# Block-sparse attention and a gated MLP in one kernel: transposing the probabilities of 28 jobs and of the all-key groups with VectorE blocks and transfers within SBUF

## The chip, the cores and the metric

One core of one Trainium2 chip runs the whole program in one launch. The metric is the device time of one execution in microseconds (us). A time of the program is the median of several executions; the profile is of one more execution, and it has a time of its own.

## What is computed

The inputs are q, k and v of shape (4, 8, 768, 64): 4 batches, 8 heads, 768 tokens, 64 columns, in float32. Tokens are cut into 24 blocks of 32. A query block attends to the blocks beside it, to the first and the last block, and to 3 sampled blocks; the first and the last query block attend to all 24. The attended rows go through an MLP without bias, with a gate.

```python
scores = scale * np.matmul(q, k.transpose(0, 1, 3, 2))
mask = np.abs(blk_i - blk_j) <= window
mask = mask | (blk_i == 0) | (blk_j == 0) | (blk_i == n_blocks - 1) | (blk_j == n_blocks - 1)
for qb in range(n_blocks):
    for kb in sampled_blocks[qb]:
        mask[qb * block:(qb + 1) * block, kb * block:(kb + 1) * block] = True
...
attn = np.exp(scores)
attn = attn / (np.sum(attn, axis=-1, keepdims=True) + 1e-09)
attn_out = np.matmul(attn, v)
...
h = x @ w_in            # (3072, 512) @ (512, 2048)
g = h * np.clip(h + 3.0, 0.0, 6.0) / 6.0
out = g @ w_out         # (3072, 2048) @ (2048, 512)
```

## The kernel before

**Units of work.** Attention is done in 24 groups (`GROUPS`), each of two batches and two query blocks. 22 of them are sparse: a group gives two jobs (class `Job`, L452), one for each batch, so there are 44 jobs, numbered 0 to 43. A job holds 2 query blocks of all 8 heads against 8 key blocks each. The two other groups hold the first and the last query block, which see all keys: each gives four pieces of dense work (class `Dense`, L536), so there are 8, numbered 0 to 7. A dense piece works in two halves of 384 keys.

**A job, step by step.** `s` (L462) writes scores with TensorE into two PSUM banks; `mx` takes the negated maxima with VectorE; `e` (L479) is four exponentials of ScalarE of 128x256, which write the probabilities `p` with the keys of a chunk interleaved (an inner step of 4 elements). Probabilities then stand with queries on the partitions, and the product with V needs keys there. So `t` (L486) turns them: four TensorE transposes of 128x128 against `ident` into a third PSUM bank, twice per job, and `ca` (ScalarE) or `cv` (VectorE) copies each bank to SBUF as `pT`. `av` (L499) multiplies with V: 16 small matmuls of 32 output rows each, twice per job, into the bank `small` (the trace shows each of these float32 matmuls, and those of `s`, as two). `dn` and `ml` divide, `x` transposes the 128x256 result in blocks of 32x32 with VectorE, `xh` and `xl` split it into two parts of float32r for the MLP.

**A dense piece** has the same steps, with four sets of three transposes (`t`, L572, twice per half) and `av` with 64 output rows per matmul. Its `x` (L617) is 8 small TensorE matmuls against `ident` into `small` (16 in the trace).

**The MLP** is 96 steps (class `Step`, L658): 6 units of 512 tokens by 16 slices of the hidden width. `h` is 12 matmuls of 128x512 in two halves, `o` 12 more in four parts. `wh` (ScalarE) and `wl` (GpSimd, now and then VectorE) split a weight slice; `ga`, `gb`, `gh`, `gl` make the gated hidden slice and split it. A unit starts when 4 groups of attention are done. Weights are loaded and unpacked once, in 32 pieces (class `Weight`), in the first 200 us or so. Keys and values of a group are gathered into one of two `kp` and `vp` buffers (class `Cache`, L377; `RING = 2`).

**What sets the order.** The order is written out by hand in one list, `SCORE` (L44): phrases such as `j36 e_10 e_11` name the work and its operations. Every operation is issued in this order through a helper at L316, so each engine runs its own operations strictly in the list's order, and nearly every row of a trace has the line L316. Most transfers go through one queue, SyncE's (SP). Where an operation on an engine waits, everything behind it on that engine waits too.

**Buffers the change touches.** `p` and `pT`: 3 buffers of 512 columns each. `WBUFS = (3, 2)`: buffers of the split `w_in` and `w_out` slices. `EARLY = 4`: jobs of the first 4 groups use the banks that `o` needs later (`OUT`) for scores and transposes.

Of the kernel before, what the change touches and what calls it, by code (L numbers as in the profile page):

```python
# [10 lines left out]
F32 = mybir.dt.float32  # L11
# [3 lines left out]
ALU = mybir.AluOpType  # L15
# [19 lines left out]
EARLY = 4  # L35
WBUFS = (3, 2)
# [8 lines left out]
    k0 samp_1; q1 load_0; k0 table_1; c0 kg_0; q0 load_1; c1 vw_01; c0 kw_11 vg_0; w1 load_1; c0 kr_111 kr_001; c1  # L45
    kw_11 vw_00 kf_0; c0 vw_01 kw_00; c1 kc_1; k0 index; w0 load_0; c1 kr_000; w1 size; q0 qs_0; c1 kr_010; c0 vw_02
    vw_00; k0 ident_0; c0 vr_01; j1 s; j0 s; j1 mx_0; c0 vr_00; j1 mx_1; c2 kc_0; j0 mx_0; w0 size; j0 mx_1; j1 e_00;
    c1 vr_00; w0 bits_0; j0 e_00 e_01; j1 e_01; j0 e_10; c1 vw_02; j0 e_11; q1 qs_0; w2 load_0; c2 kr_010; j2 s; j0
    t_0 t_1; c2 kr_000; j0 cv_0 ca_1; j1 t_0; j0 av_0; j1 e_10 cv_0 e_11; j0 av_1; j2 mx_0; c2 kw_01; j3 s; j0 dn; j2
    e_00; j0 ml; j2 e_01 mx_1; j1 t_1; c3 kw_01; j3 mx_0; j2 t_0; c1 vg_0; w0 bits_1; q2 load_0; j1 av_0; j2 ca_0; c1  # L50
    vr_01; j3 mx_1; j2 e_10; j1 cv_1; j3 e_00; j2 e_11; w1 bits_0; j1 av_1; j3 e_01; w1 bits_1; w2 size; j2 t_1; c2
    vw_00; w0 bits_2; c3 kr_010; j2 ca_1; j1 dn; j0 x; j3 e_10; j1 ml; w1 bits_2; j1 x; q3 load_0; c2 vw_02; q2 qs_0;
    w4 load_0; m0 wh_0; j4 s; c2 vr_01; j3 e_11; m0 wl_00; j1 xh; m0 wh_1; j2 av_0; j1 xl_1; c2 vw_01; j0 xh; j5 s; c3
    kc_1; c2 vr_00; w2 bits_0; j3 t_0; j5 mx_0; c3 kr_000; j3 t_1; j0 xl_1; j5 e_00; j2 av_1; j4 mx_0 e_00; j2 dn; q3
    qs_0; j2 ml; q4 load_0; j3 ca_0 cv_1; j4 e_01; j3 av_0; w2 bits_1; w4 size; j3 av_1; j2 x; j5 e_01; m0 wl_11; j4
    t_0; c3 vw_00; j4 mx_1; c4 kw_01; j4 ca_0; w3 load_0; j3 dn; j4 e_10; c3 vr_01; w2 bits_2; j4 e_11; j3 ml; j4 t_1;
    j5 mx_1; j4 av_0; c3 vw_01; j4 cv_1; j5 t_0; c3 vw_02; j3 x; c3 vr_00; j6 s; j5 e_10; j2 xh; j5 e_11; j2 xl_0; j5
    ca_0; j4 av_1; c4 kw_00; j6 mx_0; c4 kr_000; j5 t_1; w4 bits_0; j6 e_00; j4 dn; j6 e_01; j7 s; j5 cv_1; j3 xh; w3
    size; j6 mx_1 t_0; c4 kr_010; j4 ml; j6 e_10; j3 xl_1; j5 av_0; j6 ca_0; j7 mx_0; j6 e_11; j5 av_1; w3 bits_0; j7
    e_00; w3 bits_1; j7 e_01; w6 load_0; j7 t_0; w3 bits_2; j6 t_1; j5 dn; j7 mx_1; j4 x; j7 e_10; w4 bits_1; j6 ca_1;  # L60
    q4 qs_0; j5 ml; w4 bits_2; j6 av_0; j7 ca_0; j6 av_1; j5 x; j7 e_11; w5 load_0; j4 xh; j7 t_1; c5 kw_00; j6 dn; j5
    xh; j4 xl_0; c4 vw_01; j6 ml; j7 ca_1; j8 s; w7 load_0; j5 xl_0; j6 x; m1 wh_0; c4 vw_02 vw_00; j7 av_0; j6 xh; m1
    wl_00; j8 mx_0; c4 vr_00; m2 wh_0; j7 av_1; j8 e_00; j7 dn; j8 e_01; j7 ml; j8 t_0; c4 vr_01; j7 x; j6 xl_1; j7
    xh; w6 size; j7 xl_1; j8 mx_1; m0 h_0; w5 size; j8 e_10; w5 bits_0; j8 e_11; w6 bits_0; m0 h_1; m1 wh_1; j8 cv_0;
    m1 wl_11; j8 t_1; m0 ga; w6 bits_1; j8 ca_1; w6 bits_2; j9 s; m0 gb; w9 load_0; q5 load_0; w5 bits_1; m0 gh; m1
    h_0; c5 kw_01; w5 bits_2; w7 size; m0 gl; j9 mx_0; w8 load_0; m1 h_1; c5 kr_000; m2 wl_01; j9 e_00 e_01; w7
    bits_0; m0 o_0; m1 ga; j8 av_0; m1 gb; w9 size; j8 av_1; c5 kr_010; j9 mx_1; m3 wh_0; j9 t_0; m2 h_0; w7 bits_1;
    m3 wl_00; j9 e_10 e_11; w7 bits_2; m1 gh; m0 o_1; m1 gl; m2 h_1; w9 bits_0; w10 load_0; c5 vw_00 vw_01; m0 o_2; j8
    dn; m2 ga; w9 bits_1; m0 o_3; w8 size; w9 bits_2; j9 t_1 ca_0; m1 o_0; j8 ml; w11 load_0; q5 qs_0; j9 cv_1; c5
    vr_01; m1 o_1; w8 bits_0; j10 s; m2 gb; c6 kw_00; m2 gh; j9 av_0; c5 vw_02; j10 mx_0; m2 wh_1; j9 av_1; m2 gl; c5  # L70
    vr_00; j10 mx_1; m1 o_2; w10 size; w8 bits_1; j10 e_00; m1 o_3; j10 e_01; m2 wl_11; j10 e_10; m3 h_0; j10 e_11; w8
    bits_2; w10 bits_0; m4 wh_0; w12 load_0; m3 h_1; j8 x; w11 size; w10 bits_1; j10 t_0; m4 wl_01; m3 ga; m2 o_0; w10
    bits_2; j10 t_1; j9 dn; w14 load_0; m2 o_1; w11 bits_0; j10 ca_1; m3 gb; m2 o_2; j8 xh; j10 ca_0; w11 bits_1; m4
    h_0; m5 wh_0; j9 ml; w11 bits_2; m3 wh_1; j11 s; m3 gh; w13 load_0; c6 kr_010; m3 gl; j10 av_0; j11 mx_0; j10
    av_1; j11 mx_1; m4 h_1; j11 e_00; w12 size; m5 wl_01; j11 e_01; q6 load_0; m3 wl_11; j11 e_10; m2 o_3; c6 kr_000;
    m4 ga; w12 bits_0; m3 o_0; w14 size; m4 gb; m3 o_1; j11 e_11; w12 bits_1; m4 gh; j11 t_0; w12 bits_2; c6 kw_01; m5
    h_0; m4 gl; j11 ca_0; j10 dn; w16 load_0; j9 x; w13 size; c6 vr_01; j11 t_1; w13 bits_0; m5 h_1; w14 bits_0; j11
    ca_1; w14 bits_1; m4 wh_1; m3 o_2; w14 bits_2; m6 wh_0; j10 ml; m5 ga; m3 o_3; w15 load_0; m4 wl_11; q6 qs_0; j11
# [215 lines left out]
def fused_kernel(ctx: ExitStack, tc, qT, kG, vG, vP, kD, vD, sampled, w_in, w_out, table, ident_d, out):  # L294
# [42 lines left out]
    class Index(Work):  # L337
# [99 lines left out]
    class Group(Work):  # L437
# [347 lines left out]
```

## Time and profile before

| what | value |
|---|---|
| median of 3 executions | 771.0 us (770.13 to 771.55) |
| the profiled execution's own time | 768.11 us |
| its span, from first to last instruction | 766.3 us |
| TensorE busy | 724.3 us, 95% of the span |
| VectorE / ScalarE / GpSimd busy | 45% / 56% / 47% |
| granted TensorE clock, mean of the span | 0.994 |
| moved by DMA | 102.52 MB, mean 134 GB/s |

The profiled execution is 2.9 us below the median of the others. Busy time counts an instruction from its start to its modelled end; TensorE's instructions overlap, so what a matmul costs is read from the distance between the starts of neighbours, not from its own duration. `PE` is TensorE's matmul, `PEld` its weight load, DVE is VectorE, ACT ScalarE, POOL GpSimd, SP the queue of SyncE.

### The profile page before, as it was taken

How to read it: one execution, taken by the hardware profiler on the slowest of the kernel's cores; microseconds unless marked ns; L12 is line 12 of the kernel's file. 1: busy time of each engine (PE TensorE's matmuls, PEld its weight loads, DVE VectorE, ACT ScalarE, POOL GpSimd, SP SyncE). 2: the span in 40 equal slices, each digit the busy share in tenths (PEclk: the TensorE clock that was granted, in tenths of full speed). 3: DMA queues.
4: the chain of work that ended last, by engine and by line, in shares of the span. 5: the costliest groups of instructions: out<-in, count | busy, mean ns of one | idle time of the engine just before them, and what ended most of it. 6: DMA issues, size and time to landing. Idle time of an engine off the chain costs nothing.

```text
span 766.3 us, 18861 instructions
## 1 busy us (share of the span) xinstructions
PE 724.3 (95%) x7616; PEld 558.4 (73%) x7616; DVE 341.7 (45%) x698; ACT 426.4 (56%) x790; POOL 360.7 (47%) x291
## 2 busy tenths in 40 slices
PE   1577999999999999999999999999999999999997
PEld 0344777777777777777778777777777777888885
DVE  2567989895443434542323334436642133221112
ACT  1567678766565445645656554455654645544441
POOL 0011324355446434455664663442546564676663
PEclk9989999999999999999999999999999999999999
DMA  8688878776361553223451144533442600010001
GB/s 281 199 274 253 284 232 246 239 249 198 122 197 62 169 176 124 64 74 115 153 161 58 35 138 129 179 131 106 133 142 86 207 20 2 1 56 1 0 1 55
DMA packets 57866, 102.52 MB, mean 134 GB/s; under 512 B 7859, under 2 KB 36148, under 8 KB 57780
## 3 DMA queue, kind: packets, MB, share of 16 engines
q1 hardware_dynamic: 56512, 99.62, 41.3%
q10 hardware_dynamic: 1268, 1.71, 0.6%
q8 instruction: 60, 0.98, 0.5%
q14 instruction: 26, 0.21, 0.1%
HBM read 95.00 MB, written 6.29 MB: 132 GB/s over the span
## 4 chain that ended last, share of the span: by engine, by line
PE 89%; SPq 4%; DMA 2%; DVE 2%; ACT 1%; issue 1%; ACTq 0%; POOL 0%; POOLq 0%; DVEq 0%
PE hid L316 35%; PE out L316 34%; PE bank L316 12%; PE small L316 8%; SPq L316 3%; DMA stage<-w_out 1%; ACT p L316 1%; SPq L370 1%; DVE m L316 0%; DMA stage<-w_in 0%; DMA kp<-kG 0%; ACT g L316 0%; DMA vp<-vG 0%; DMA out_dram<-stage 0%; DVE w_in L316 0%
## 5 line engine op out<-in xcount | busy, mean ns | idle before, releaser
L316 PE MATMUL hid<-x,whi 128*128 128x512 f32 x768 | 242.9, 397 | 0.3 <-ACT x L316 0.2
L316 POOL TENSOR_TENSOR glo<-g,ghi 128x512 fp32r<-128x512 f32 x96 | 126.5, 1318 | 181.8 <-ACT ghi L316 163.6
L316 DVE SCALAR_TENSOR_TENSOR g<-g,hid 128x512 f32<-128x512 f32 x96 | 65.8, 686 | 229.8 <-ACT g L316 229.8
L316 PEld LDWEIGHTS hid<-x,whi 128*128 128x128 f32 x768 | 140.6, 188 | 34.6 <-issue 3.2
L316 POOL TENSOR_TENSOR wlo<-w_out,whi 128x512 fp32r<-128x512 f32 x87 | 113.7, 1308 | 98.0 <-ACT whi L316 78.3
L316 PE MATMUL out<-whi,ghi 128*128 128x512 f32 x384 | 159.7, 416 | 0.0
L316 ACT ACTIVATE p<-bank,m 128x256 f32<-128x256 f32 (+1 forms) x192 | 120.8, 691 | 65.1 <-DVE m L316 64.5
L316 POOL TENSOR_TENSOR wlo<-w_in,whi 128x512 fp32r<-128x512 f32 x87 | 113.4, 1308 | 84.3 <-ACT whi L316 79.7
L316 PE MATMUL out<-whi,glo 128*128 128x512 f32 x384 | 150.5, 392 | 0.2 <-POOL glo L316 0.2
L316 PE MATMUL hid<-x,wlo 128*128 128x512 f32 x384 | 150.2, 391 | 0.0
L316 PE MATMUL out<-wlo,ghi 128*128 128x512 f32 x384 | 150.0, 391 | 0.0
L316 ACT ACTIVATE g<-hid,half_b 128x512 f32<-128x512 f32 x96 | 66.1, 688 | 122.8 <-PE hid L316 93.1
L316 DVE TENSOR_REDUCE m<-bank 128x2 f32<-128x512 f32 (+1 forms) x112 | 70.3, 645 | 61.0 <-PE bank L316 60.9
L316 PEld LDWEIGHTS out<-whi,ghi 128*128 128x128 f32 x384 | 72.1, 188 | 22.9 <-issue 9.5
L316 PEld LDWEIGHTS out<-whi,glo 128*128 128x128 f32 x384 | 72.1, 188 | 16.5 <-POOL glo L316 0.6
L316 PEld LDWEIGHTS hid<-x,wlo 128*128 128x128 f32 x384 | 72.1, 188 | 15.8
L316 PEld LDWEIGHTS out<-wlo,ghi 128*128 128x128 f32 x384 | 72.4, 189 | 11.6
L316 ACT CAST whi<-w_out 128x512 fp32r<-128x512 f32 x96 | 60.0, 625 | 32.5 <-PE out L316 29.2
L316 ACT CAST ghi<-g 128x512 fp32r<-128x512 f32 x96 | 60.0, 625 | 31.9 <-DVE g L316 17.2
L316 ACT CAST whi<-w_in 128x512 fp32r<-128x512 f32 x96 | 59.6, 624 | 12.9 <-PE hid L316 8.3
L316 PE MATMUL bank<-ident,p 128*128 128x128 f32 x384 | 58.2, 274 | 2.0 <-ACT p L316 1.7
L316 PEld LDWEIGHTS small<-vp,pT 128*32 128x32 f32 x2816 | 42.6, 110 | 22.9 <-issue 15.3
(59 smaller groups left out, 607.4 us busy)
## 6 DMA issues: line engine op xcount, KB each, us to landing
vp<-vG SPq DMA_DIRECT2D x176, 130.0 KB, 3.4
kp<-kG SPq DMA_DIRECT2D x129, 128.0 KB, 2.8
kp<-kG SPq DMA_DIRECT2D x42, 256.0 KB, 3.6
stage<-w_in SPq DMA_DIRECT2D x16, 512.0 KB, 3.9
stage<-w_out SPq DMA_DIRECT2D x15, 512.0 KB, 4.3
vp<-vP SPq DMA_DIRECT2D x26, 260.0 KB, 3.9
stage<-vD SPq DMA_DIRECT2D x16, 390.0 KB, 4.0
out_dram<-stage SPq DMA_DIRECT2D x24, 256.0 KB, 2.9
```

The lines of the kernel that those rows point to most:

```text
L316: return lambda *a, **k: tc.keep_in_program_order(op(*a, **k))
L370: loads, values = nc.values_load_multi_w_load_instructions(row, engines=[engines[q]], min_val=0, max_val=NB - 1, skip_runtime_bounds_check ...
```

## The change

Jobs 16 to 43 (28 jobs, `MOVED = 16`) and all 8 dense pieces no longer use TensorE to turn the probabilities. `e` writes into one tile `p` of 1024 columns, with the 4 slots of a chunk outermost. `tr` (VectorE) transposes each 32x32 block in place, in two instructions of 128x512 per job (128x384 per dense half, also two). `mv` then issues four transfers on SP: transfer t reads 32 partitions of `p` in 4 segments and writes 128 partitions of `pT`, 256 columns (1 KB) each; a dense half moves 192 columns. `av` reads its weights from the new places. A dense `av` now has 32 output rows per matmul (twice as many matmuls), and the host lays V out for it in another order. The dense `x` is done by VectorE.

Jobs 0 to 15 keep `t`, `ca` and `cv`. Their `s` now writes PSUM with the keys interleaved (an inner step of 4 elements), and `e` reads and writes in one run of 256. `p` and `pT` have 2 buffers of 1024 columns, `WBUFS` is (2, 2), `EARLY` is 3. `SCORE` is a new list; the order of jobs among MLP steps is nearly the old one.

```diff
-EARLY = 4
-WBUFS = (3, 2)
+EARLY = 3
+MOVED = 16
+WBUFS = (2, 2)
...
+    def move(out, in_, width):
+        for t in range(4):
+            dma.dma_start(out=out[:, t * width:(t + 1) * width],
+                          in_=in_[32 * t:32 * t + 32, :4 * width].rearrange("p (s n) -> p s n", s=4))
...
     class Job(Work):
...
-                        pe.matmul(self.ps[y][32 * t:32 * t + 32, 256 * x:256 * x + 256], lhsT=self.group.q[half, t, at:at + 32],
-                                  rhs=self.k[half, 4 * x:4 * x + 8, self.b, BLK * t:BLK * t + BLK], start=True, stop=True)
+                        keys = self.k[half, 4 * x:4 * x + 8, self.b, BLK * t:BLK * t + BLK]
+                        to = self.ps[y][32 * t:32 * t + 32, 256 * x:256 * x + 256]
+                        if not self.moved:
+                            to, keys = to.rearrange("p (c k s) -> p c s k", c=2, s=4), keys.rearrange("p (c s) k -> p c s k", c=2)
+                        pe.matmul(to, lhsT=self.group.q[half, t, at:at + 32], rhs=keys, start=True, stop=True)
...
         def e(self, y, x):
...
+            out, in_ = self.pr[:, 512 * y + 256 * x:512 * y + 256 * x + 256], self.ps[y][:, 256 * x:256 * x + 256]
+            if self.moved:
+                out = self.pr.rearrange("p (s y x c k) -> p y x c s k", s=4, y=2, x=2, c=2)[:, y, x]
+                in_ = in_.rearrange("p (c s k) -> p c s k", c=2, s=4)
...
+        def tr(self, i):
+            half = self.pr[:, 512 * i:512 * i + 512]
+            dve.transpose(out=half, in_=half)
+
+        def mv(self):
+            self.prT = sb.tile([P, 1024], F32, name="pT", bufs=2)
+            move(self.prT, self.pr, 256)
...
     class Dense(Work):
...
-        def t(self, y, half):
-            self.pt[y, half] = bank()
-            for c in range(3):
-                pe.transpose(self.pt[y, half][:, c * P:c * P + P], self.pr[y, half][:, c * P:c * P + P], ident)
...
+        def tr(self, i, half):
+            part = self.pr[half][:, 384 * i:384 * i + 384]
+            dve.transpose(out=part, in_=part)
+
+        def mv(self, half):
+            self.prT[half] = sb.tile([P, 1024], F32, name="pT", bufs=2)[:, :768]
+            move(self.prT[half], self.pr[half], 192)
...
-            for k in range(NKC):
-                for x in range(2):
-                    pe.matmul(self.xt[BLK * x:BLK * x + BLK, k], lhsT=flat[:, BLK * k:BLK * k + BLK], rhs=ident[:, 64 * x:64 * x + 64],
-                              start=True, stop=True)
+            for x in range(2):
+                for z in range(2):
+                    dve.transpose(out=self.xt[64 * self.u + 32 * x:64 * self.u + 32 * x + 32, z].rearrange("p k n -> p (k n)"),
+                                  in_=self.xq[64 * x + 32 * z:64 * x + 32 * z + 32].rearrange("p h d -> p (h d)"))
```

**Where instructions stand now, TensorE.** The first place is a job in the second half of the program, about MLP step 63. The rows are TensorE's instructions in order: `hid` is `h` of a step, `out_78` to `out_81` are the four parts of an `o`, `bank<-kp` the scores of a job, `bank<-ident,p` a set of four transposes, `small<-vp,pT` the product with V. Before, behind the scores of job 36 and an `h`:

```order
L316 MATMUL out_78<-whi_7240,ghi 128x512
L316 MATMUL out_78<-wlo_7248,ghi 128x512
L316 MATMUL out_78<-whi_7240,glo 128x512
L316 MATMUL bank<-ident,p 128x128 x4
L316 MATMUL out_79<-whi_7240,ghi 128x512
L316 MATMUL out_79<-wlo_7248,ghi 128x512
L316 MATMUL out_79<-whi_7240,glo 128x512
L316 MATMUL bank<-ident,p 128x128 x4
L316 MATMUL out_80<-whi_7240,ghi 128x512
L316 MATMUL out_80<-wlo_7248,ghi 128x512
L316 MATMUL out_80<-whi_7240,glo 128x512
L316 MATMUL small<-vp_74,pT 32x65 x32
```

Now the same engine, at the scores of job 36, with the product of job 34 right behind them:

```order
L315 MATMUL bank<-kp_72,q 32x256 x16
L315 MATMUL small<-vp_75,pT 32x65 x32
L315 MATMUL out_81<-whi_6846,ghi 128x512
L315 MATMUL out_81<-wlo_6906,ghi 128x512
L315 MATMUL out_81<-whi_6846,glo 128x512
L315 MATMUL out_78<-whi_7013,ghi 128x512
L315 MATMUL out_78<-wlo_7118,ghi 128x512
L315 MATMUL out_78<-whi_7013,glo 128x512
```

The two sets of transposes are gone, and the product with V stands two jobs behind the scores instead of in the same job's turn.

**The tightest place, TensorE.** Dense piece 3 (about MLP step 31) issues the scores of both halves at once; from there to its first product with V (`small<-stage,pT`) TensorE has 27 `out` matmuls and the scores of one job. These are the last rows of that stretch, and the product's two parts:

```order
L315 MATMUL out_81<-whi_4039,ghi 128x512
L315 MATMUL out_81<-wlo_4061,ghi 128x512
L315 MATMUL out_81<-whi_4039,glo 128x512
L315 MATMUL out_78<-whi_4163,ghi 128x512
L315 MATMUL out_78<-wlo_4168,ghi 128x512
L315 MATMUL out_78<-whi_4163,glo 128x512
L315 MATMUL out_79<-whi_4163,ghi 128x512
L315 MATMUL out_79<-wlo_4168,ghi 128x512
L315 MATMUL out_79<-whi_4163,glo 128x512
L315 MATMUL small<-stage,pT 32x65 x24
L315 MATMUL bank<-kp_73,q 32x256 x16
L315 MATMUL small<-stage,pT 32x65 x24
```

What moved here is all that TensorE did for the turning of the probabilities: none of it is left between scores and product.

**The queue of SP, at the same dense pieces (2 and 3).** `pT<-p` are the new transfers, 4 for a half, 8 where both halves follow each other; the rest are loads:

```order
L315 DMA stage<-vD 128x780
L315 DMA kp_72<-kG 128x2x256
L315 DMA stage<-vD 128x780
L315 DMA pT<-p 128x1x192 x8
L315 DMA stage<-kD 128x768 x2
L315 DMA stage<-vD 128x780
L315 DMA kp_73<-kG 128x2x256
L315 DMA vp_75<-vP 64x1040
L315 DMA stage<-vD 128x780
L315 DMA pT<-p 128x1x192 x8
L315 DMA q<-qT 128x512
```

The loads stand as they did; the new transfers stand between them, behind loads of up to 390 KB and ahead of the next piece's keys.

## Rows read from the trace of the kernel before

**Rows 1.** The page: busy time, share of the span and count by engine, and the span in 40 slices of 19.2 us (busy tenths, granted clock in tenths).

```profile
PE 724.3 (95%) x7616; PEld 558.4 (73%) x7616; DVE 341.7 (45%) x698; ACT 426.4 (56%) x790; POOL 360.7 (47%) x291
PE   1577999999999999999999999999999999999997
PEclk9989999999999999999999999999999999999999
```

**Rows 2.** Busy time by stretches of the span: from:to, length, then busy us (instructions) of PE, PEld, DVE, ACT, POOL, then the granted clock, the share of DMA time and GB/s.

```profile
0.00:20.00 20.00, 3.67 (x64) 1.78 (x64) 4.95 (x15) 4.65 (x8) 0.28 (x5) 1.00 0.83 273
20.00:60.00 40.00, 25.08 (x630) 16.44 (x630) 24.00 (x54) 25.63 (x49) 2.02 (x2) 0.91 0.77 239
60.00:100.00 40.00, 35.43 (x550) 26.07 (x553) 31.82 (x63) 27.44 (x51) 10.53 (x8) 1.00 0.84 268
100.00:150.00 50.00, 50.00 (x552) 38.69 (x541) 45.61 (x81) 38.93 (x71) 18.40 (x14) 1.00 0.76 238
300.00:350.00 50.00, 50.00 (x577) 38.03 (x576) 22.66 (x50) 27.51 (x52) 24.05 (x19) 1.00 0.31 97
500.00:550.00 50.00, 49.53 (x684) 36.84 (x684) 25.09 (x55) 30.44 (x58) 20.18 (x16) 1.00 0.39 120
```

**Rows 3.** The page: the chain of work that ended last, shares of the span by line.

```profile
PE hid L316 35%; PE out L316 34%; PE bank L316 12%; PE small L316 8%; SPq L316 3%; DMA stage<-w_out 1%; ACT p L316 1%; SPq L370 1%; DVE m L316 0%; DMA stage<-w_in 0%; DMA kp<-kG 0%; ACT g L316 0%; DMA vp<-vG 0%; DMA out_dram<-stage 0%; DVE w_in L316 0%
```

**Rows 4.** TensorE in order of time, from 302.51 us: start, us until the last one of the row ends, the operation and how many.

```profile
304.00 0.49 PE L316 MATMUL bank<-ident,p 128*128 128x128 f32 x3
304.25 0.71 PE L316 MATMUL hid<-x,whi 128*128 128x512 f32 x2
...
305.72 0.49 PE L316 MATMUL bank<-ident,p 128*128 128x128 f32 x3
305.97 0.48 PE L316 MATMUL out<-whi,ghi 128*128 128x512 f32 x1
306.29 0.39 PE L316 MATMUL out<-wlo,ghi 128*128 128x512 f32 x1
306.52 0.39 PE L316 MATMUL out<-whi,glo 128*128 128x512 f32 x1
...
313.63 0.64 PE L316 MATMUL small<-ident,xq 128*32 128x64 f32 x16
314.20 0.50 PE L316 MATMUL out<-whi,ghi 128*128 128x512 f32 x1
314.54 0.39 PE L316 MATMUL out<-wlo,ghi 128*128 128x512 f32 x1
...
323.61 1.03 PE L316 MATMUL bank<-ident,p 128*128 128x128 f32 x8
324.40 0.48 PE L316 MATMUL out<-whi,ghi 128*128 128x512 f32 x1
324.71 0.39 PE L316 MATMUL out<-wlo,ghi 128*128 128x512 f32 x1
...
325.97 1.09 PE L316 MATMUL bank<-kp,q 64*32 64x256 f32 x32
326.99 1.12 PE L316 MATMUL small<-vp,pT 128*32 128x65 f32 x64
328.04 0.50 PE L316 MATMUL out<-whi,ghi 128*128 128x512 f32 x1
```

**Rows 5.** Groups of instructions of one shape: count | busy us, mean ns of one | idle time of the engine just before them, and what ended it.

```profile
L316 PE MATMUL bank<-ident,p 128*128 128x128 f32 x384 | 58.2, 274 | 2.0 <-ACT p L316 1.7
L316 DVE STREAM_TRANSPOSE xt<-xq 128x256 f32<-128x256 f32 x44 | 19.1, 434 | 0.7 <-POOL x L316 0.4
L316 DVE TENSOR_REDUCE m<-bank 128x2 f32<-128x512 f32 x80 | 53.5, 682 | 27.5 <-PE bank L316 27.4
L316 ACT ACTIVATE p<-bank,m 128x256 f32<-128x256 f32 x160 | 103.0, 713 | 46.9 <-DVE m L316 46.5 <-DVE rec L316 0.2
L316 ACT ACTIVATE p<-bank,m 128x384 f32<-128x384 f32 x32 | 17.9, 580 | 18.2 <-DVE m L316 18.0
```

**Rows 6.** The page: transfers by tile, queue and count, KB each, median us from issue to landing.

```profile
vp<-vG SPq DMA_DIRECT2D x176, 130.0 KB, 3.4
kp<-kG SPq DMA_DIRECT2D x129, 128.0 KB, 2.8
stage<-vD SPq DMA_DIRECT2D x16, 390.0 KB, 4.0
```

**Rows 7.** The queue of SP in order of time: start, us in which the row's issues ran, the transfer and how many.

```profile
322.96 1.40 SPq L316 DMA_DIRECT2D kp<-kG  x3
...
527.12 3.78 SPq L316 DMA_DIRECT2D kp<-kG  x6
```

**Rows 8.** TensorE in order of time, from the first instruction to the first MLP matmul: start, us, operation, count, and in brackets the idle time before it and what ended it.

```profile
14.55 1.96 PE L316 MATMUL out<-kp,q 64*32 64x256 f32 x32 [14.55 <-DMA kp<-kG]
...
39.85 1.96 PE L316 MATMUL bank<-kp,q 64*32 64x256 f32 x32 [5.89 <-DMA vp<-vG]
...
70.04 1.02 PE L316 MATMUL hid<-x,whi 128*128 128x512 f32 x2 [0.22 <-ACT x L316]
```

More of the change, by code (lines that the diff above doesn't have):

```diff
@@ L50 @@
[L50 to L54, printed above, removed]
@@ L459, in __init__ @@
             self.c0 = self.group.c0 + 64 * s
-            self.early = group < EARLY
+            self.early, self.moved = group < EARLY, n >= MOVED
         def s(self):
@@ L488, in t, with part @@
             for c in range(4):
-                pe.transpose(self.pt[y][:, c * P:c * P + P], self.pr[y][:, c * P:c * P + P], ident)
+                pe.transpose(self.pt[y][:, c * P:c * P + P], self.pr[:, 512 * y + c * P:512 * y + c * P + P], ident)
+        def part(self, y):
+            if y == 0:
+                self.prT = sb.tile([P, 1024], F32, name="pT", bufs=2)
+            return self.prT[:, 512 * y:512 * y + 512]
         def ca(self, y):
-            self.prT[y] = sb.tile([P, 512], F32, name="pT", bufs=3)
-            act.copy(out=self.prT[y], in_=self.pt[y])
+            act.copy(out=self.part(y), in_=self.pt[y])
         def cv(self, y):
-            self.prT[y] = sb.tile([P, 512], F32, name="pT", bufs=3)
-            dve.tensor_copy(out=self.prT[y], in_=self.pt[y])
+            dve.tensor_copy(out=self.part(y), in_=self.pt[y])
         def av(self, y):
@@ L588, in av @@
             for c in range(3):
-                for x in range(2):
-                    at, to = ((3 * half + c) * 2 + y) * VW, (2 * half + y) * VW
-                    pe.matmul(self.us[64 * x:64 * x + 64, to:to + VW], lhsT=self.prT[y, half][:, c * P + 64 * x:c * P + 64 * x + 64],
-                              rhs=self.v[x][:, at:at + VW], start=c == 0, stop=c == 2)
+                at, to = ((3 * half + c) * 2 + y) * VW, (2 * half + y) * VW
+                for t in range(4):
+                    col = BLK * (6 * t + 3 * y + c)
+                    pe.matmul(self.us[32 * t:32 * t + 32, to:to + VW], lhsT=self.prT[half][:, col:col + BLK],
+                              rhs=self.v[t // 2][:, at:at + VW], start=c == 0, stop=c == 2)
         def fd(self):
-            self.f = sb.tile([P, 4], F32, name="f", bufs=1)
+            self.f = sb.tile([P, 4], F32, name="f", bufs=2)
             dve.tensor_tensor(out=self.f[:, 0:2], in0=self.m[:, 0:2], in1=self.m[:, 2:4], op=ALU.min)
@@ L630, in xh, with xl @@
             act.copy(out=dst(0), in_=src)
-        def xl(self):
+        def xl(self, engine):
             src, dst = self.ends()
-            dve.tensor_tensor(out=dst(1), in0=src, in1=dst(0).bitcast(F32), op=ALU.subtract)
+            (dve if engine else pool).tensor_tensor(out=dst(1), in0=src, in1=dst(0).bitcast(F32), op=ALU.subtract)
     class Weight(Work):
@@ L753, in layouts @@
         "kD": kb.transpose(0, 1, 2, 5, 3, 4).reshape(B, HP, P, S),
[L754 removed]
+        "vD": vo.reshape(B, HP, 2, 6, 4, BLK, VW).transpose(0, 1, 5, 4, 3, 2, 6).reshape(B, HP, P, 6 * 2 * VW),
         "sampled": np.ascontiguousarray(np.asarray(sampled_blocks)).view(np.int32).reshape(1, 2 * NB * NR),
```

489 lines of the change are left out of this document (243 added, 246 removed).

## The prediction

> **What bounds the kernel now.** I read the busy shares first, then the stretches, then the chain. TensorE is busy 95% of the span, and in the 40 slices its digit is 9 almost everywhere; the granted clock is 9 tenths or more but for one early slice, so this is work at the 2.4 GHz level [rows 1]. The stretches say where the rest is: TensorE is idle for 16.3, 14.9 and 4.6 us in the first three (35.8 us in the first 100), and from 100 us on it is full, 50.00 of 50 us, while VectorE, ScalarE and GpSimd are busy 40 to 61% in the later stretches [rows 2]. The chain that ended last agrees: 89% of the span are four TensorE groups, 69% the MLP, 12% the scores and transposes in `bank`, 8% the small products [rows 3]. So from 100 us to the end the time is the sum of TensorE's work, and what is taken from it comes off the total, as long as no other engine or transfer is late. The first MLP matmul starts at 70.04 us, behind waits for keys and values [rows 8]; that start is ruled by loads.
>
> **What goes from TensorE.** Neighbouring starts give the price. Eight transposes take from 323.61 to 324.40, 0.79 us; the `out` matmul behind them then takes 0.31 instead of the usual 0.23 to its neighbour, so 0.87 for two sets, 0.435 a set [rows 4]. The 28 jobs lose 2 sets each: 56 x 0.435 = 24.4 us. A set of three takes 0.25, and the matmul behind it 0.32 instead of 0.23: 0.34 [rows 4]. The dense pieces lose 4 sets each: 32 x 0.34 = 10.9 us. A dense `x` takes 0.57 and the matmul behind it 0.34 instead of 0.23: 0.68 [rows 4], times 8 is 5.4 us. Sum: **40.7 us**. Bounds: without the dearer neighbour, 56 x 0.395 + 32 x 0.25 + 8 x 0.57 = 34.7; with the group's busy time, 58.2 / 384 = 0.152 a transpose [rows 5], 320 x 0.152 + 5.4 = 54. I take 40.7, since starts show what a full engine gives up, and busy time counts overlap twice.
>
> **What comes to TensorE.** A dense `av` becomes 96 matmuls in the trace's count, of the form whose 64 take 1.05 us (326.99 to 328.04) [rows 4]: 1.6 us, about what the 48 wider ones take now; I cost it at nothing. The scores of jobs 0 to 15 now write PSUM with a step of 4 elements. No row shows such a write by TensorE. Nothing, if it writes a column at a time wherever it lands; twice the 1.02 us of a job's scores (325.97 to 326.99) [rows 4] if it suffers, 16 us in all, less what falls into the idle first 100 us. ScalarE does suffer from the stepped write: 713 ns for 256 columns against 580 for 384 in one run [rows 5]. I take nothing for TensorE, whose columns are one element per partition, and keep 16 as an end. A gain has no place here.
>
> **What comes to VectorE, and goes from ScalarE.** A block transpose of 256 columns takes 434 ns [rows 5]; 512 columns lie between 0.68 (a reduction over 512 [rows 5]) and 0.87 (twice 434). I take 0.75: 56 x 0.75 + 32 x 0.6 = 61 us more on VectorE, against copies of `pT` that go. In the later stretches it has 25 to 27 of 50 us free [rows 2], about 250 us in all, so TensorE's work hides it. ScalarE loses copies and has shorter exponentials, since they no longer write with a step. The Trainium skill, "VectorE: DVE Perf Modes", section "Rules for kernel authors", sends a 128x128 transpose to TensorE where PSUM will do as the target; that weighs one transpose by itself, and would keep the 40.7 us where they are. Here the rows decide against it: the engine it names is the full one.
>
> **The moves.** This is where the gain can be lost. 28 jobs and 16 dense halves each issue four transfers, 176 issues on SP. Issues stand 0.47 us apart in a plain run (three in 1.40 us) and 0.63 with register loads (six in 3.78) [rows 7]. A load of the same form, 128 rows of 1 KB, lands in 2.8 us [rows 6]. So a move takes 3 x 0.47 + 2.8 = 4.2 us. Bounds: 2.8 if they overlap fully, 4 x 3.4 = 13.6 if they ran one after another at the pace of a V row load [rows 6]. I take 4.2, as the nearest row has the same shape. SP has no compute behind it, but loads of the next keys and values queue behind each move, and a move waits for its `tr`. The new order has room for that. At the tightest place, dense piece 3, TensorE has 27 matmuls of 0.23 and 1.02 us of scores, some 7.3 us, before the product. The chain needs two maxima and the last exponential, 0.57 each, 0.6 for the last `tr`, and 4.2: 6.5 us. The second half follows after 1.5 us more of TensorE's work, but needs its own maxima (1.1) and four more issues (1.9): late by 0.7 us. Job 36 has about 16 us of TensorE's work between scores and product, against 0.68 + 4 x 0.71 + 0.75 + 4.2 = 8.5. So most jobs are safe and the dense halves have little room: I take 3 us of waits in all; 0 is one end, and 16 halves late by 1.2 us (a 390 KB load in front, 4.0 instead of 2.8 [rows 6]), 19 us, the other.
>
> **The start.** One weight load fewer stands ahead of the last values of the fourth cache: 512 KB at 250 GB/s [rows 2], 2 us earlier. The fewer banks for early jobs and the shorter exponentials of jobs 0 to 7 (64 x some 0.2 us on ScalarE, mostly under the loads) I let cancel. The start may shift by 4 us either way.
>
> **Sum.** 768.1 for the profiled execution: - 40.7 - 2 + 3 = 728.4. That execution is 2.9 us below the median of 771.0, so the median becomes **731**.
>
> **Rivals.**
> *The moves land late* (slower). If the four transfers of a move do not overlap, or read slowly out of 32 partitions, each product with V stops TensorE, and with it everything. From 10 us a move even the roomier jobs are short. The point from which it decides is a mean lateness of 39.7 / 44 = 0.9 us a move; with 2 us the time is 731 - 3 + 88 = 816. For it: no row shows a transfer within SBUF. Against it: the same shape lands in 2.8 us, and SP's other loads do overlap. Beside this, the Trainium skill, "VectorE: DVE Perf Modes", section "The three transpose paths", warns that a plain copy which transposes by strides is 19 times slower where the destination's inner stride is large. By that rule this rival would be certain if the transfers turned single elements; here they carry runs of 256, since VectorE turns the blocks. Chance 0.05.
> *SP's queue gets in the way* (a smaller gain). About 14 groups' keys and values are still loaded after job 16, in a queue where now up to 34 issues fall into 20 us, 17 us at 0.5 [rows 7]. If each group's last load comes 1 to 1.5 us late, 14 to 21 us return: 745 to 752. For it: SP waits in order. Against it: from 100 us on TensorE hardly waits for a load now. Chance 0.13.
> *The stepped scores cost* up to 16 us, of which half is under the start's loads: 739 to 747. Chance 0.06.
> *No gain* because something equal takes over, GpSimd for instance, with 24 of 50 us busy [rows 2]: 768 to 772. Nothing in the rows speaks for it. Chance 0.03.
>
> **The numbers.** My forecast (720 to 742) has 0.73; with most of the second and third rival the range is 720 to 750. A measurement of this kernel can tell 0.2%, 1.5 us, from no change: faster 0.93, within it 0.02, slower 0.05.
>
> **What would show it.** Right: TensorE's matmul groups `bank<-ident,p` shrink to the 16 first jobs' sets, the starts between MLP matmuls stay 0.23, VectorE's new transposes take 0.7 to 0.9 us, TensorE is full after 100 us, and the first MLP matmul starts at 66 to 72 us. Wrong: idle time of TensorE ended by a DMA into `pT`, most at dense pieces, a landing above 5 us for `pT<-p`, scores of jobs 0 to 15 longer than 1.02 us, or waits for `kp` and `vp` after 200 us.

## The result, and the profile after

| | before | after |
|---|---|---|
| median | 771.27 us (770.13 to 771.78) | 741.15 us (738.75 to 743.29), 4 runs |
| profiled execution | 768.1 us | 743.04 us, span 741.3 us |

The ratio is 0.961 [0.957, 0.965]: 30 us faster, where 40 were forecast. 741 lies within 720 to 750, 10 us above 731: a quarter of the forecast gain is missing.

The page of the changed kernel, busy time and slices (18.5 us each), beside [rows 1]:

```profile
PE 697.3 (94%) x7552; PEld 529.3 (71%) x7552; DVE 381.9 (52%) x781; ACT 373.0 (50%) x734; POOL 369.5 (50%) x296
PE   2756999999999999899999999999999999999997
PEclk9777999999999999999999999999999999999999
```

TensorE is still the full engine; it lost 27 us of busy time, about what the span lost. VectorE gained 40 us, ScalarE lost 53. In the second to fourth slice the granted clock stands at 7 tenths.

Stretches of the changed kernel, columns as in [rows 2]:

```profile
20.00:60.00 40.00, 28.68 (x628) 20.14 (x628) 21.14 (x49) 21.18 (x47) 0.00 (x0) 0.75 0.76 235
60.00:100.00 40.00, 34.50 (x463) 26.40 (x464) 31.58 (x66) 23.80 (x49) 6.29 (x5) 0.87 0.73 238
300.00:350.00 50.00, 49.07 (x640) 35.44 (x633) 27.06 (x59) 25.23 (x53) 24.31 (x19) 1.00 0.63 178
500.00:550.00 50.00, 48.59 (x752) 35.97 (x751) 32.78 (x72) 27.50 (x60) 25.21 (x20) 1.00 0.64 174
```

The later stretches are no longer quite full (49.07 and 48.59 of 50 us), and the share of DMA time there is 0.63 and 0.64, where it was 0.31 and 0.39.

Groups of one shape in the changed kernel, columns as in [rows 5]:

```profile
L315 ACT ACTIVATE p<-bank,m 128x256 f32<-128x256 f32 x164 | 71.7, 475 | 57.2 <-DVE m L315 48.3 <-PE out L315 4.6 <-issue 2.6
L315 DVE STREAM_TRANSPOSE p<-p 128x512 f32<-128x512 f32 x56 | 37.9, 695 | 15.0 <-ACT p L315 14.5 <-DMA kp<-kG 0.2 <-DMA vp<-vG 0.2
...
L315 DVE STREAM_TRANSPOSE p<-p 128x384 f32<-128x384 f32 x32 | 16.9, 559 | 8.5 <-ACT p L315 6.0 <-DMA pT<-p 1.5 <-DMA kp<-kG 0.8
L315 PE MATMUL bank<-ident,p 128*128 128x128 f32 x80 | 13.0, 291 | 3.9 <-ACT p L315 2.3 <-DVE w_in L315 1.7
```

The new transposes take 0.70 and 0.56 us (0.75 and 0.6 forecast), the exponentials 475 ns instead of 713, and of 384 `bank<-ident,p` 80 are left.

The transfers within SBUF, beside the loads of [rows 6] (KB each, median us from issue to landing):

```profile
vp<-vG SPq DMA_DIRECT2D x175, 130.0 KB, 3.3
kp<-kG SPq DMA_DIRECT2D x129, 128.0 KB, 2.6
pT<-p SPq DMA_DIRECT2D x112, 128.0 KB, 2.8
...
pT<-p SPq DMA_DIRECT2D x64, 96.0 KB, 2.6
```

128 KB land in 2.8 us, as the nearest row had it, and the two loads shown beside them are no slower than before; key loads of 256 KB went from 3.6 to 4.0 us.

What TensorE waited for from 100 us to the end of the changed kernel (us in total, times, longest):

```profile
PE small L315 <- DMA pT<-p: 2.2, 5, 0.8
PE bank L315 <- DMA kp<-kG: 1.4, 1, 1.4
PE bank L315 <- ACT p L315: 1.3, 1, 1.3
PE bank L315 <- DVE rec L315: 0.9, 1, 0.9
PE hid L315 <- DVE g L315: 0.8, 2, 0.6
PE out L315 <- POOL glo L315: 0.2, 1, 0.2
```

Seven microseconds of waits, 2.2 of them for the moves. No engine or transfer has taken TensorE's place, so waits alone do not explain the missing 10 us.

### The profile page after: what moved, and what is told of

It reads as the page before. It is cut to its first block, busy times and chain, and to the rows that moved or that the text cites. A ratio compares the mean times of both kernels' runs of the same rounds, so it can differ in the third digit from the quotient of the medians.

```text
span 741.3 us, 19139 instructions
## 1 busy us (share of the span) xinstructions
PE 697.3 (94%) x7552; PEld 529.3 (71%) x7552; DVE 381.9 (52%) x781; ACT 373.0 (50%) x734; POOL 369.5 (50%) x296
## 4 chain that ended last, share of the span: by engine, by line
PE 80%; SPq 6%; DVE 5%; DMA 4%; ACT 2%; issue 2%; ACTq 0%; POOL 0%; POOLq 0%; DVEq 0%
PE hid L315 34%; PE out L315 33%; PE bank L315 8%; PE small L315 6%; SPq L315 5%; DMA kp<-kG 1%; DMA vp<-vG 1%; DVE w_in L315 1%; DMA q<-qT 1%; DMA pT<-p 1%; DVE m L315 1%; SPq L369 1%; DVE g L315 1%; ACT p L315 1%; ACT g L315 0%
## 5 line engine op out<-in xcount | busy, mean ns | idle before, releaser
L315 PE MATMUL hid<-x,whi 128*128 128x512 f32 x768 | 245.6, 400 | 1.2 <-DVE g L315 0.8
L315 PEld LDWEIGHTS hid<-x,whi 128*128 128x128 f32 x768 | 142.3, 188 | 40.5 <-issue 3.0
L315 POOL TENSOR_TENSOR wlo<-w_out,whi 128x512 fp32r<-128x512 f32 x88 | 116.5, 1324 | 82.0 <-ACT whi L315 65.9
L315 PE MATMUL out<-whi,ghi 128*128 128x512 f32 x384 | 155.5, 405 | 0.0
L315 PE MATMUL hid<-x,wlo 128*128 128x512 f32 x384 | 152.0, 396 | 0.0
L315 POOL TENSOR_TENSOR wlo<-w_in,whi 128x512 fp32r<-128x512 f32 x89 | 117.3, 1321 | 58.6 <-ACT whi L315 39.0
L315 ACT ACTIVATE p<-bank,m 128x256 f32<-128x256 f32 (+1 forms) x196 | 89.1, 492 | 72.0 <-DVE m L315 63.0
L315 ACT CAST ghi<-g 128x512 fp32r<-128x512 f32 x96 | 59.5, 620 | 34.3 <-DVE g L315 22.1
L315 ACT CAST whi<-w_in 128x512 fp32r<-128x512 f32 x96 | 59.3, 617 | 28.1 <-PE hid L315 20.0
L315 PE MATMUL bank<-kp,q 64*32 64x256 f32 x1312 | 49.3, 406 | 18.9 <-DMA vp<-vG 11.7
L315 DVE STREAM_TRANSPOSE p<-p 128x512 f32<-128x512 f32 (+1 forms) x88 | 54.8, 645 | 23.5 <-ACT p L315 20.5
```

The lines of the kernel that those rows point to most:

```text
L315: return lambda *a, **k: tc.keep_in_program_order(op(*a, **k))
```

## The experiments

**The two kernels again, on one chip.** `b_again` is the kernel before, one execution; `a_again` is the changed kernel.

> The kernel before, profiled beside the others. In the first pair of profiles the MLP matmuls of 128x512 start 227 ns apart before and some 230.5 ns after, also in the last 70 us where nothing else differs. Theory A (the pace belongs to the execution, not to the change): this profile may show anything from 227 to 231 ns, and the changed kernel beside it the same. Theory B (the moves' traffic or VectorE's transposes slow TensorE): 227 ns here, 230 ns in the changed kernel. Time 770 to 772 us with 227 ns, up to 778 us with 230 ns.

> The changed kernel again. Theory A: the time lies between 737 and 743 us and goes with the pace of the profile, 227 ns at 737, 230.5 ns at 743. Theory B: 230 ns and some 741 us again. Both: idle time of TensorE after 100 us near 7 us, first MLP matmul at 72 to 74 us.

Measured: 770.0 (span 768.2) and 740.41 us (739.22 to 743.93; span 739.4), ratio 0.961 [0.959, 0.964]. Two spans from one chip can be taken apart: from each start on TensorE to the next, from 100 us to the end, idle time set aside, summed by group (us, each good to some 0.3):

| group | b_again | a_again |
|---|---|---|
| `bank<-ident,p` | 34.3 | 3.6 |
| `small<-ident,xq` | 4.6 | 0 |
| `out<-whi,ghi` | 94.6 | 90.6 |
| all `hid` | 258.0 | 262.3 |
| the other two `out` | 174.1 | 175.2 |
| scores and products with V | 96.0 | 96.7 |
| idle | 0.9 | 6.0 |
| sum | 662.5 | 634.4 |

What was to go went, but the `hid` matmuls, none of which the change touches, became dearer by 4.4 us. The next rows show how, TensorE in order of time near the end (start, us, operation, count), where only MLP work is left. The kernel before, run again:

```profile
693.17 0.61 PE L316 MATMUL hid<-x,whi 128*128 128x512 f32 x2
693.63 0.39 PE L316 MATMUL hid<-x,wlo 128*128 128x512 f32 x1
693.85 0.61 PE L316 MATMUL hid<-x,whi 128*128 128x512 f32 x2
694.31 0.39 PE L316 MATMUL hid<-x,wlo 128*128 128x512 f32 x1
694.53 0.39 PE L316 MATMUL out<-whi,ghi 128*128 128x512 f32 x1
```

The changed kernel, its first profile:

```profile
692.33 0.63 PE L315 MATMUL hid<-x,whi 128*128 128x512 f32 x2
692.80 0.39 PE L315 MATMUL hid<-x,wlo 128*128 128x512 f32 x1
693.03 0.63 PE L315 MATMUL hid<-x,whi 128*128 128x512 f32 x2
693.50 0.39 PE L315 MATMUL hid<-x,wlo 128*128 128x512 f32 x1
693.73 0.39 PE L315 MATMUL out<-whi,ghi 128*128 128x512 f32 x1
```

Six `hid` matmuls take 1.36 us (227 ns each) before and 1.40 (233 ns) after, with the same weights, shapes and granted clock, and no attention work beside them. Three theories: this execution of the chip (A), the new transfers' traffic (B), or where the operands lie (C). A falls here already: on one chip, `b_again` has 227 and `a_again` 233. (The expectations below call a fourth one D: the new order of the matmuls, or the fewer buffers of split weights.)

**Without the transfers.** The moved jobs and dense halves read the weights that job 15 left, so the 176 issues go, and with them the products' wait.

```diff
-            self.prT = sb.tile([P, 1024], F32, name="pT", bufs=2)
-            move(self.prT, self.pr, 256)
+            self.prT = jobs[15].prT
...
```

> The changed kernel with the transfers within SBUF left out: the products of the moved jobs and of the dense pieces read the weights that job 15 left, so SP has 176 issues and 21 MB less, and no product waits for a move. Theory A: only the waits go that end at a move or behind SP's queue, 3 to 6 us: some 735 us, the pace as in the repeat beside it. Theory B: pace back to 227 ns as well, 11 to 14 us less, some 728 us. If the moves had been late by the 0.9 us each of the rival: 40 us less.

Measured: 736.91 us, ratio 0.957 [0.955, 0.959]: 3.5 us under `a_again`. The moves cost that much in all, issues, traffic and lateness together. TensorE's idle time after 100 us is 3.3 us here instead of 6.0: the waits for `pT<-p` (1.3 us) are gone, and so is the one for `kp<-kG` (1.4 us), which the moves had caused. The group `hid<-x,wlo` has a mean of 396 ns in this run, as in the changed kernel's profile, and 391 in `b_again`. B falls: 21 MB fewer transfers leave the pace as it was.

**The transposes back on TensorE, as added work.** Sets of four ahead of each half's product in the moved jobs, sets of three in the dense halves, into a spare corner of PSUM.

```diff
         def av(self, y):
+            if self.moved:
+                for c in range(4):
+                    pe.transpose(self.us[:, 384:512], self.prT[:, 512 * y + c * P:512 * y + c * P + P], ident)
...
```

> The changed kernel with as many TensorE transposes put back as it lost (4 in front of each product of a moved job, 3 in front of each of a dense half), into unused columns of the product's bank, with nobody reading them: this is the price of the transposes alone. By the starts (0.435 us a set of four, 0.34 a set of three): 56 x 0.435 + 32 x 0.34 = 35 us more. By the group's busy time (0.152 us each): 49 us more. If TensorE had hidden them: nothing.

Measured: 787.84 us, ratio 1.022 [1.020, 1.025], 47.4 us over `a_again`. That is above the 35 us that the sets' starts had given in the kernel before. TensorE in order of time in this run:

```profile
198.22 1.09 PE L315 MATMUL bank<-kp,q 64*32 64x256 f32 x32
199.25 0.66 PE L315 MATMUL small<-ident,pT 128*128 128x128 f32 x4
199.83 0.66 PE L315 MATMUL small<-vp,pT 128*32 128x65 f32 x32
```

A set of four takes 0.58 us here (199.25 to 199.83), where two sets took 0.79 in the kernel before [rows 4]: it stands between two groups of 32-column matmuls. The kernel before has this price too, at its start, where a set stands between such groups (52.57 to 53.16):

```profile
52.57 0.66 PE L316 MATMUL out<-ident,p 128*128 128x128 f32 x4
53.16 1.09 PE L316 MATMUL bank<-kp,q 64*32 64x256 f32 x32
```

A transpose's price depends on what it stands between, so this run does not by itself give the price of those that were removed.

**Where the operands lie.** The change gives `m` four buffers instead of two (32 bytes each here). The tiles allocated behind it, `whi`, `wlo`, `g`, `ghi` and `glo` (and `xq` and `xt`, which no MLP matmul reads), therefore start 64 bytes off: the first `whi` buffer of the `w_out` side at byte 209,920 of a partition before (205 x 1024) and at 209,984 after, `g` at 218,112 and 218,176. `aligned` moves the small tile `rec` into a pool of its own at the end, so these five start on multiples of 1024 again; order and arithmetic stay.

```diff
+    late = ctx.enter_context(tc.tile_pool(name="late", bufs=2))
...
-            self.rec = sb.tile([P, 4], F32, name="rec")
+            self.rec = late.tile([P, 4], F32, name="rec")
...
```

> The changed kernel with the small tile rec moved to the end of SBUF. In the changed kernel two more buffers of the maxima m (32 bytes each) stand in front of the split weights and the gated hidden slices, so all of these start 64 bytes further than a multiple of 1024 bytes; before, and with this edit, they start on one. Nothing else changes. Theory C (TensorE reads operands slower from the shifted addresses): MLP matmuls again start 227 ns apart instead of 230.5, and the time falls by 6 to 9 us, to some 733 us. Theory A (the pace belongs to the execution) is already against the repeat of both kernels on one chip. Theory D (the pace comes from the order of the matmuls, or from fewer buffers of split weights): no change, 740 us.

Measured: **732.68 us** (730.15 to 735.35), ratio 0.950 [0.947, 0.952], 7.7 us under `a_again`. TensorE in order of time in this run:

```profile
692.55 0.62 PE L316 MATMUL hid<-x,whi 128*128 128x512 f32 x2
...
693.91 0.39 PE L316 MATMUL out<-whi,ghi 128*128 128x512 f32 x1
```

Six again take 1.36 us (692.55 to 693.91). This version beats both kernels.

**The same shift in the kernel before, and other shifts.** `before_shifted` is the kernel before with four buffers of `m`; `shift128` and `shift256` are the changed kernel with more buffers of `rec`, so that the five tiles stand 128 and 256 bytes off a multiple of 1024.

```diff
-                self.m = sb.tile([P, 4], F32, name="m")
+                self.m = sb.tile([P, 4], F32, name="m", bufs=4)
...
```

```diff
-            self.rec = sb.tile([P, 4], F32, name="rec")
+            self.rec = sb.tile([P, 4], F32, name="rec", bufs=4)
...
```

(`bufs=8` for 256 bytes.)

> The kernel before with four buffers of m instead of two, which moves its split weights and hidden slices to the 64 bytes behind a multiple of 1024 that the changed kernel has. Theory C: MLP matmuls start 230 to 231 ns apart and the time rises by 7 to 9 us, to some 778 us. Theory D: no change, 770 to 771 us.

> The changed kernel with four buffers of rec instead of two, so the split weights and hidden slices start 128 bytes behind a multiple of 1024 instead of 64. Theory C, if what counts is a multiple of 128: 227 ns and some 733 us; if it needs more than that: 230 ns and 740 us. Theory D: 740 us.

> The changed kernel with eight buffers of rec, so that the split weights and hidden slices start 256 bytes behind a multiple of 1024 (64 in the changed kernel, 128 in the earlier run, 0 in the aligned one). If a multiple of 256 is enough: MLP matmuls 227 ns apart and some 733 us. If it takes 512 or more: 230 ns and 737 to 741 us.

The pace below is the mean from start to start after 300 us, over unbroken stretches of `hid` or of `out` that stand between MLP matmuls (300 to 470 of each):

| kernel | tiles off 1024 by | median us | ratio to the kernel before, same chip | `hid` ns | `out` ns |
|---|---|---|---|---|---|
| b_again | 0 | 770.0 | | 227.3 | 226.8 |
| before_shifted | 64 B | 777.59 | 1.009 [1.006, 1.012] | 233.3 | 229.6 |
| a_again | 64 B | 740.41 | 0.961 [0.959, 0.964] | 233.3 | 228.9 |
| shift128 | 128 B | 737.9 | 0.956 [0.953, 0.958] | 232.2 | 228.4 |
| shift256 | 256 B | 732.72 | 0.948 [0.944, 0.953] | 226.9 | 226.8 |
| aligned | 0 | 732.68 | 0.950 [0.947, 0.952] | 226.9 | 226.8 |

The same group in `shift128`:

```profile
L315 PE MATMUL hid<-x,wlo 128*128 128x512 f32 x384 | 152.2, 396 | 0.0
```

and in `shift256`:

```profile
L315 PE MATMUL hid<-x,wlo 128*128 128x512 f32 x384 | 150.2, 391 | 0.0
```

C is shown from both sides: the shift alone costs the kernel before 6.7 us (777.59 against 770.94, the median of the kernel before on that chip), and undoing it gives the changed kernel 7.7. (These two medians come from two chips; by the ratios it is 8 to 9.) D falls with it: `aligned` keeps the order and the buffers of the split weights. 64 and 128 bytes are slow, 256 is as good as 0.

**The rest of the operands aligned too.** `x`, `kp` and some constants, `x` only at a multiple of 512 so far, go to multiples of 1024 as well, by creating three small constants earlier and `VP` later.

```diff
+    half_b = const.tile([P, 1], F32, name="half_b")
+    raw_t = const.tile([1, 2 * NB * NR], I32, name="raw")
+    blocks_t = const.tile([1, NB, NR], I32, name="blocks")
...
```

> The aligned kernel with the small constant tiles first and the V buffers last, so that the MLP's input x, the keys and the loaded weights also start on a multiple of 1024 bytes; x started on a multiple of 512 until now. If a multiple of 512 is enough for an operand, or if only the split weights and hidden slices count: no change, 731 to 734 us. If x suffers as well: the hid matmuls come closer and up to 1152 x 0.006 = 7 us go.

Measured: 733.51 us, ratio 0.953 [0.950, 0.955], the pace 226.9 and 226.8 ns. Nothing more is to be had from these tiles.

**The transposes back, together.** On `aligned`, eight (six for a dense half) in one group ahead of the first product, as the two sets of a job stood behind each other in [rows 4].

```diff
+                if self.moved:
+                    for c in range(8):
+                        pe.transpose(self.us[:, 384:512], self.prT[:, c * P:c * P + P], ident)
...
```

> The aligned kernel with the lost TensorE transposes put back as in the earlier run, but all 8 (6) of a product in one group ahead of its first half, so that the halves of the product are not pulled apart. If the price of a set is its own 0.35 to 0.40 us and each further change between small and full matmuls costs some 0.1 to 0.17: 28 x 0.87 + 16 x 0.68 = 35 us more than the aligned kernel, some 768 us, against 47 us in the earlier run. If a transposition costs 0.145 us wherever it stands: 47 us more again, 780 us.

Measured: 767.17 us, ratio 0.996 [0.994, 0.997], 34.5 over `aligned`. TensorE in order of time in this run:

```profile
184.84 0.39 PE L316 MATMUL out<-whi,glo 128*128 128x512 f32 x1
185.07 1.03 PE L316 MATMUL small<-ident,pT 128*128 128x128 f32 x8
186.04 1.11 PE L316 MATMUL small<-vp,pT 128*32 128x65 f32 x64
```

Eight take 0.97 us, not 1.16 (two times 0.58). After 100 us the 320 take 40.3 us by their starts, idle time is 3.6 us less than in `aligned`, and the other groups together 2.4 us less: 34.3. That comes near what the sets of the kernel before gave, 24.4 + 10.9, but in part by luck: the transposes themselves take 5 us more than that here, and less waiting and cheaper neighbours take it back.

**The moves from ScalarE's queue.** Is SP, with no compute of its own, what keeps the moves cheap?

```diff
-            dma.dma_start(out=out[:, t * width:(t + 1) * width],
+            act.dma_start(out=out[:, t * width:(t + 1) * width],
```

> The changed kernel with the 176 transfers of the moves issued from ScalarE's queue instead of SP's. If SP's queue holds the moves or the loads up: 1 to 4 us less (leaving the moves out altogether gave 3.5). If ScalarE's issues and its waits for tr hold up the exponentials and the hidden slices behind them: slower, by up to 176 x 0.06 = 10 us of ScalarE's time where it bites, or more where it waits for VectorE.

Measured: 769.98 us (762.36 to 773.62), ratio 0.997 [0.994, 1.000]: 29.6 over `a_again`, the whole gain. The waits of this run, all engines, and ScalarE's queue at one of them:

```profile
ACT g L315 <- DMA pT<-p: 24.8, 7, 4.1
...
PE hid L315 <- DVE g L315: 12.0, 11, 2.3
...
370.33 2.52 ACTq L315 DMA_DIRECT2D pT<-p  x4
374.44 0.69 ACT L315 ACTIVATE g<-hid,half_b 128x512 f32<-128x512 f32 x1 [4.12 <-DMA pT<-p]
```

ScalarE stops in front of `g`, the MLP's activation, behind moves: of the 4.12 us here, 2.52 are its own four issues. An issue takes 0.62 us of ScalarE's queue by the median, 109 us for 176; no run shows the 0.06 us of the expectation. VectorE's `g` then comes late for TensorE. TensorE's idle time after 100 us grows from 6.0 to 25.2 us. Some 10 us more of the 29.6 are spread over dearer matmul groups and are not explained.

**The moves twice.** On `aligned`, each move is issued twice into the same tile; the second set follows the first.

```diff
-        for t in range(4):
+        for t in (0, 1, 2, 3, 0, 1, 2, 3):
```

> The aligned kernel with each move issued twice into the same tile; the second set waits for the first to land, so a move lands some 4 us later, and SP has 176 issues and 21 MB more. This is the slower rival made true. The forecast gave the products 4 to 12 us between the issue of a move and TensorE's arrival, and priced every microsecond beyond that in full: with a mean spare time of 2 to 3 us, 44 x 1 to 2 us, 45 to 90 us more, 778 to 820 us. If the spare time is larger than 4 us nearly everywhere: less than 15 us more.

Measured: 828.25 us, ratio 1.076 [1.074, 1.079], 95.6 over `aligned`, more than was expected of any case. TensorE's waits in this run, the longest sum:

```profile
PE small L316 <- DMA pT<-p: 36.8, 47, 3.3
```

and the page's landings of the same run:

```profile
pT<-p SPq DMA_DIRECT2D x224, 128.0 KB, 2.7
```

By the median a transfer lands as fast as ever, but 47 products now wait, 0.8 us each. After 100 us the span grows by 91 us against `aligned`, taken apart by starts as above: 49 are more idle time, 24 dearer products with V, 14 dearer MLP matmuls and 4 dearer scores. Much of the dearer work is the clock's. TensorE in order of time in this run, and the stretch around it, columns as in [rows 2]:

```profile
514.61 0.42 PE L316 MATMUL small<-stage,pT 128*32 128x65 f32 x2 [3.24 <-DMA pT<-p]
...
517.92 1.22 PE L316 MATMUL hid<-x,whi 128*128 128x512 f32 x2
518.94 0.63 PE L316 MATMUL hid<-x,wlo 128*128 128x512 f32 x1
...
500.00:600.00 100.00, 85.09 (x914) 61.29 (x911) 50.11 (x117) 39.07 (x81) 38.97 (x32) 0.91 0.60 165
```

TensorE waits 3.24 us for the second moves, and the granted clock falls to 1.2 GHz: the two `hid` matmuls behind the product take 1.02 us (517.92 to 518.94) instead of 0.46. Between 100 us and the last 5 us TensorE has 61 us at that level, where `aligned` has none; at the full clock's prices the work in them would have taken some 30 us less (an estimate from the starts at either level). The schedule has room for one move, not for two, and a late move costs more than its wait. Of the moves' price it shows one thing: 3.5 us is what they cost in the room that the order gives them.

**Not tried.** The jobs' real transposes on TensorE within the new order, so that nothing is left out, and the waits kept with the transfers alone removed: neither fitted the order and the buffers.

## Why the prediction was right, and where it failed

**What goes from TensorE: right, mechanism and size.** Forecast 40.7 us. With `aligned` in place of `a_again`, where the pace is the same as before, the starts give `bank<-ident,p` 34.3 to 3.5 (30.8), `small<-ident,xq` 4.6, `out<-whi,ghi` 94.6 to 90.4 (4.3, the dearer matmul behind a set) and the `hid` 258.0 to 256.4 (1.6): 41.3 us. Taking neighbouring starts rather than busy time was the right choice. The end of 54, from busy time, was too high for these places, although `transposes_added` shows that the same sets, without the dense `x`, can cost 47 elsewhere.

**The moves: right in price by luck, wrong in place.** They land in 2.8 us, an issue takes 0.60 us of SP by the median where issues 0.47 us apart were forecast, and they cost 3.5 us by `no_transfers` against 3 forecast. Idle time after 100 us rose by 5.2 (0.9 to 6.0), of which 1.3 us in four waits are for `pT<-p` in `a_again`. These are not at dense pieces, as forecast, but at jobs between 531 and 543 us; the 3 us were taken for dense pieces, so that the sums agree is luck. The rival that the moves are late falls: the mean lateness is 3.5 / 44 = 0.08 us a move, against 0.9 from which it decides. One landing in the first profile took 5.2 us, above the 5 named as a sign of being wrong, the next 4.9; in `a_again` the longest took 4.5. Had the rival come true, its price of one microsecond for each microsecond of lateness would have been too low: in `moves_twice` the clock fell as well. The page "VectorE: DVE Perf Modes" of the Trainium skill, section "The three transpose paths", warns of a plain DMA copy that transposes by strides, 19 times slower than the DMA's own transpose where the destination's inner stride is large; no run here has such a copy, and runs of 1 KB showed no slowness.

**SP's queue: fell, but for 1.4 us.** From 100 us on, `a_again` waits once for a load, 1.4 us for `kp<-kG` at 189 us, and `no_transfers` does not. `moves_act` adds why the queue matters: the same transfers cost 30 us on a queue whose engine has work for the MLP.

**The stepped scores: cost nothing, as taken.** TensorE in order of time in the changed kernel's profile, about the first MLP matmuls:

```profile
72.79 0.48 PE L315 MATMUL hid<-x,whi 128*128 128x512 f32 x1
...
78.34 1.09 PE L315 MATMUL bank<-kp,q 64*32 64x256 f32 x32
79.36 1.11 PE L315 MATMUL small<-vp,pT 128*32 128x65 f32 x64
```

A job's 32 scores take 1.02 us (78.34 to 79.36), as in [rows 4].

**The dense `av`: nothing, as taken.** Twice as many matmuls take 12.3 us where the wider ones took 13.5.

**The start: wrong by some 2 us.** Forecast 2 us earlier. The first MLP matmul came at 72.79 us in this profile, and at 73.26 in `a_again` against 72.42 in `b_again`: later than the 66 to 72 us named as a sign of being right. The two spans differ by 28.8 us and the parts after 100 us by 28.1, so the start gave 0.7. Its spread from run to run hides more than that: the granted clock from 20 to 60 us is 0.75 in one execution of the changed kernel and 0.91 in another.

**The pace: the step that failed.** The sum took the MLP matmuls' 0.23 us as given, and "what would show it" said that they "stay 0.23". To that digit they did: 0.227 and 0.233 read alike in a column of starts. But 1152 `hid` and 1152 `out` at 6.0 and 2.1 ns (a_again against b_again) would be 9.3 us; by the medians of `aligned` and `a_again` it is 7.7, and by the starts of all of them after 100 us 7.6, so those that stand beside other work lose less than those in unbroken stretches. The cause stands in an edit that the prediction did not price at all, two more buffers of a 32-byte tile. That 741 still falls into the forecast range is luck in part: the range was made for late moves, loads and stepped scores, and of the missing 10 us these took little.

The account from 768.2 to 739.4: -41.3 (removed), +5.2 (waits), +7.6 (pace, `hid` and `out` after 100 us, a_again against aligned), +0.4 (scores and products 0.7 more, the other `out` 0.3 less), -0.7 (start): -28.8. With the pace put right, 732.7 was measured where 731 was forecast; the waits are 2 us more than the sum has, and the start gave 1 us less.

**VectorE and ScalarE: hidden, as taken.** 54.8 us of new block transposes (37.9 + 16.9) end no wait of TensorE after 100 us; what they delay can only lie in the waits for `pT<-p`. The Trainium skill, "VectorE: DVE Perf Modes", section "Rules for kernel authors", would send a 128x128 transpose to TensorE; `transposes_together` puts that work back there, and it costs 34.5 us. In this kernel, where TensorE is the full engine, the measurement decides against the rule.

## What to carry to other kernels

Where one engine is full, price what leaves it by neighbouring starts in its own order, and expect that price to change with the neighbours. Price every edit of a buffer count too: it moves what is allocated behind it, and the full engine's matmuls may care where their operands start, so compare the pace of untouched matmuls over long stretches and not by two digits of one start. A transfer within SBUF can replace work on a full engine if its queue belongs to an idle engine and the order leaves it room: here for one move of four transfers, not for two.

## What the runs showed of the hardware

- Matmuls of 128x512 whose split weights and hidden slices start 64 or 128 bytes off a multiple of 1024 take 232 to 233 ns instead of 227 (`hid`) and 228 to 230 instead of 227 (`out`). In `hid` only the weights moved, `x` did not. 0 and 256 bytes are equally good; 192 was not run, and what causes it is open.
- Four 128x128 transposes take 0.58 us between groups of 32-column matmuls, but eight in one group 0.97, and eight between `out` matmuls 0.79 [rows 4].
- ScalarE writes 256 columns in 475 ns in runs of 32 or 256 elements and took 713 with the earlier step of 4.
- 128 KB from 32 partitions to 128 within SBUF, in runs of 1 KB, land in 2.8 us, as a load of that size.
- Behind a wait of 3.24 us in `moves_twice` TensorE's granted clock fell to 1.2 GHz, and two `hid` matmuls took 1.02 us instead of 0.46; waits of up to 1.4 us in `a_again` left it at 2.4 GHz (granted clock 1.00 from 100 to 700 us).
- Issuing a transfer takes 0.62 us of ScalarE's queue and 0.60 us of SP's, by the median.
